# The last stores and GpSimd's last additions behind the branch of the fallback check

## The chip, the core and the metric

One core of a Trainium2 chip runs the whole program. A core has five engines with an instruction queue each: TensorE (matrix products; PE in the profile, with its weight loads as PEld), VectorE (DVE), ScalarE (ACT), GpSimd (POOL) and SyncE (SP), which here only issues transfers. Sixteen DMA engines move data between the memory of the chip and the core's own (SBUF). The metric is the time of one execution on the device in microseconds (us); lower is better.

## The reference

The input is x, 2048 rows of 512 numbers. What is computed:

```python
xn = layernorm(x)                                  # over the 512 numbers of a row
q, k, v = split(xn @ wqkv)                         # 32 heads of 16
s = softmax(q k^T / 4) v, heads joined, @ wo       # attention
h = relu(xn @ w1 + b1) ** 2                        # 512 -> 1792
g = silu(h @ w2 + b2)                              # 1792 -> 512
return x + s * g
```

## The kernel before, in words

The kernel has two ways to the result. `fast_path` computes everything, with an attention that takes no maximum out of the scores ahead of the exponential. It also gathers the smallest and largest values of what could go wrong with that (row sums, values) in a tile `stat`. At its end it makes one number of them, `nvalid`: 128 where all 128 rows of `stat` are in bounds. `general_path` reads that number into a register of every engine and branches: if it is below 128, the attention is computed again in a slow and safe manner, and the output is written over. With the inputs of the reference the number is 128, so the general path's body is passed over.

The order of the work on each engine is written out by hand. Attention goes by 64 turns (each for a group of 4 heads, a chunk of 512 queries and 8 blocks of 128 keys), and the products of the feed-forward layers are woven in between as fillers. The end of it, which the change touches, is this. The last chunk of attention is complete; VectorE adds up its two halves (line 1258), TensorE transposes the row sums into place and VectorE takes their reciprocals (1265, 1266). TensorE spreads these over the tile (1275) and VectorE multiplies (1277, 1280), which gives the normalized last head group `norms`. Two small flags are made in between (1278, 1279). Numbers are carried as a rounded part h and a rest l, so that products of rounded numbers give nearly full precision: ScalarE rounds two halves (1282), VectorE subtracts (1284). A product of the flags (1286) gives the number, and VectorE writes it to `nvalid` as an integer (1287). Then, for the last four tiles of 128 rows, three products each (1021, called from `group` at 1296) complete the projection by wo; VectorE scales each by 0.5 and multiplies it by the gate (1299); x is added (1303, 1305) and the tile is stored (1291, 1309). The additions of tiles 0 and 1 and of the first half of tile 3 are GpSimd's, those of tile 2 and the second half of tile 3 VectorE's. ScalarE's queue issues the stores of tiles 0, 2, 1 and of the first half of tile 3, in that order, SyncE's queue the store of the second half. SyncE also stores two tiles of the chunk before (1136), the last one shortly ahead of these.

Behind that each engine loads the number into a register (line 1321) and branches (1322). Line 1418 is the end of the program: SyncE waits there for all transfers, and the engines meet twice.

The tiles have fixed places in SBUF by name: `t(shape, dtype, tag)` gives the next of the places of that tag, as P0 to P15 or KA0 to KA2. The four output tiles `o` lie in P2 to P5, the rows of x that are added in KA1. The pool `sb` that holds all these is closed when `fast_path` returns.

Of the kernel before, what the change touches and what calls it, by code (L numbers as in the profile page):

```python
# [24 lines left out]
FT = mybir.dt.float32  # L25
# [23 lines left out]
def mha_ffn_kernel(ctx: ExitStack, tc: tile.TileContext, x, wqkv, wo, bx, w1, b1, w2, b2, out):  # L49
# [20 lines left out]
    gdram = dram.tile([S, D], FT, name="gd")  # L70

    with tc.tile_pool(name="sb", bufs=1) as sb, ExitStack() as banks:
        fast_path(tc, sb, banks, locals())
    general_path(tc, dram, nvalid, ident, vdram, kdram, qdram, gdram, x, wo, out)


def fast_path(tc, sb, banks, env):
# [11 lines left out]
    open_pool = lambda stack, name, side: stack.enter_context(tc.tile_pool(name=name, bufs=1, space=PSUM, side=side))  # L89
    ps = dict(B=open_pool(below, "ps0", "left"), D=open_pool(above, "ps1", "right"))  # L90

    def t(shape, dt, tag):

        cnt[0] += 1
        if tag in BUFS:
            turn[tag] = turn.get(tag, -1) + 1
            n = turn[tag] % BUFS[tag]
            p, tag = ps.get(tag), f"{tag}{places[n] if tag == 'S' else n}"
        else:
            p = None  # L100
        return (p or ps.get(tag, sb)).tile(shape, dt, tag=tag, name=f"{tag}_{cnt[0]}")

    split_tiles = [f"{a}{n}" for a in ("xh", "xl", "wf2h", "wf2l", "hh", "hl") for n in range(2)]
    for tags, n in (((f"P{i}" for i in range(16)), 1024), (("KA0", "KA1", "KA2"), 2048),
                    (("QA0", "QA1", "wf1h0", "wf1l0", *split_tiles), 1024),
# [799 lines left out]

    sums = {}

    def load_rowsums(qd, qc):
        sums[qd, qc] = t([32, 64], FT, "zc")
        sp.dma_start(sums[qd, qc], zdram[qd][qc].rearrange("h (a b) -> (h a) b", b=64))  # L910

    def rowsums(qd, qc):
        z, r = sums.pop((qd, qc)), t([32, 64], FT, "rc")
        check(z, 4 * qd + qc)
        dve.reciprocal(r, z)
        sp.dma_start(udram[qd // 2][qc][1, qd % 2].rearrange("d h (a b) -> (h a) d b", b=64),
                     r.unsqueeze(1).broadcast_to([32, 16, 64]))
# [363 lines left out]
    for n, s in enumerate(half):  # L1281
        act.copy(h[:, s], norms[n])
    for n, s in enumerate(half):
        dve.tensor_tensor(l[:, s], norms[n], h[:, s].bitcast(FT), op=OP.subtract)
    pn = acc[0:1, :1]
    mm(pn, flags[:, 0:1], flags[:, 1:2], start=True, stop=True)
    dve.tensor_copy(nvalid, pn)
    o, lins = [t([128, 512], FT, f"P{2 + i}") for i in range(4)], [two[:, 0], small[:, 1], acc, lin]
# [3 lines left out]

    late = []
    for i in range(4):
        gate, old = gsb[3, i // 2][:, i % 2], base[3, i // 2][:, i % 2]
        group(lins[i], lambda p: (h, l)[p][:, cut[i]], lambda p: wlast[0][:, p])
        for n, s in enumerate(half if i == 3 else [slice(0, 512)]):
            dst = lins[i] if i == 2 or n == 1 else o[i]
            dve.scalar_tensor_tensor(dst[:, s], lins[i][:, s], 0.5, gate[:, s], op0=OP.mult, op1=OP.mult)
            if i == 3:  # L1300
                late.append((n, dst, s, old))
            else:
                (dve if i == 2 else pool).tensor_tensor(o[i], dst, old, op=OP.add)
    for n, dst, s, old in late:
        (pool, dve)[n].tensor_tensor(o[3][:, s], dst[:, s], old[:, s], op=OP.add)
    for i in (0, 2, 1):
        save(i)
    for n, s in enumerate(half):
        (act, sp)[n].dma_start(out[1920:, s], o[3][:, s])


def general_path(tc, dram, nvalid, ident, vdram, kdram, qdram, gdram, x, wo, out):

# [7 lines left out]
    n = nc.values_load(nvalid[0:1, 0:1])  # L1321
    with tc.If(n < 128), tc.tile_pool(name="gsb", bufs=1) as sb, \
            tc.tile_pool(name="gps", bufs=1, space=PSUM) as ps:
# [51 lines left out]
        with tc.For_i(0, NK, 1) as b:  # L1375
# [17 lines left out]
            dve.tensor_tensor(gt, gt, xt, op=OP.add)  # L1393
            nc.gpsimd.dma_start(out[ds(b * 128, 128)], gt)


# [25 lines left out]
```

## Time and profile before

| | us |
|---|---|
| median of 3 runs | 1198.42 (1197.73 to 1199.0) |
| the profiled execution's own time | 1197.88 |
| its span, from first to last instruction | 1196.3 |
| TensorE busy | 1187.8 |
| ScalarE busy | 1055.8 |
| VectorE busy | 861.9 |
| GpSimd busy | 351.9 |

The profile is of one execution, taken by the hardware. Its times run from the start of the span. A row of the timeline gives start, duration, engine, the line of the kernel, the operation, what it writes and reads, and how many instructions it joins (x3); in brackets stands how long the engine sat idle before, and for whom. An engine's name with a q (ACTq, SPq, POOLq) is its instruction queue itself, which loads registers, branches and issues transfers beside the engine's work. A row of a line gives the shortest, the median and the longest duration in ns, and the first and the last start. A row of the stretches gives its bounds, its length, the busy time of TensorE, its weight loads, VectorE, ScalarE and GpSimd (with counts), the granted clock of TensorE, the share of time in which the 16 DMA engines were busy, and GB/s.

### The profile page before, as it was taken

The numbers are of one execution on the slowest core, as the hardware profiler recorded it, in microseconds if no ns is written. First come the engines' busy times: TensorE is split into PE (matmuls) and PEld (weight loads), VectorE is DVE, ScalarE is ACT, GpSimd is POOL, SyncE is SP. The second block draws the span as 40 slices with busy tenths as digits, with TensorE's granted clock in tenths as the row PEclk, the third lists the DMA queues.
The fourth block names the chain that finished last, engine by engine and source line by source line (L and its number), as shares of the span: only waits on it lengthen the run. The fifth ranks groups of instructions, "written<-read, shape, count | busy, mean of one in ns | idle before, by whom it ended". The sixth has DMA issues, their size and how long they took to land.

```text
span 1196.3 us, 24322 instructions
## 1 busy us (share of the span) xinstructions
PE 1187.8 (99%) x9853; PEld 712.3 (60%) x9853; DVE 861.9 (72%) x1367; ACT 1055.8 (88%) x1340; POOL 351.9 (29%) x209
## 2 busy tenths in 40 slices
PE   9999999999999999999999999999999999999997
PEld 6888755555555555655555655555565556555554
DVE  7666777676867777757687666677775868778876
ACT  6655689999999999999999999999999999999994
POOL 5756523040312321304032122220230403321224
PEclk9999999999999999999999999999999999999999
DMA  7798914131353223224423123141422232464344
GB/s 289 289 379 319 351 59 139 45 111 46 98 156 97 82 64 90 72 80 152 119 77 102 59 88 96 46 168 45 135 81 81 76 104 81 135 218 162 119 152 142
DMA packets 108152, 155.70 MB, mean 130 GB/s; under 512 B 43514, under 2 KB 58120, under 8 KB 108036
## 3 DMA queue, kind: packets, MB, share of 16 engines
q1 hardware_dynamic: 105108, 145.26, 37.6%
q0 software_dynamic: 2352, 7.93, 2.1%
q8 instruction: 78, 1.28, 0.5%
q10 hardware_dynamic: 576, 0.92, 0.2%
q14 instruction: 38, 0.31, 0.1%
HBM read 104.14 MB, written 49.67 MB: 129 GB/s over the span
## 4 chain that ended last, share of the span: by engine, by line
PE 99%; DVE 1%; DMA 0%; issue 0%; ACT 0%; DVEq 0%
PE acc L866 38%; PE S L568 29%; PE S L515 14%; PE B L326 5%; PE acc L515 4%; PE B L127 4%; PE lin L515 2%; PE D L326 1%; PE D L253 1%; PE S L1021 0%; PE lin L326 0%; DMA P<-in_A_x_dram 0%; PE acc L326 0%; PE S L326 0%; DVE st L190 0%; DVE T L226 0%
## 5 line engine op out<-in xcount | busy, mean ns | idle before, releaser
L519 ACT ACTIVATE P<-S 128x1024 f32<-128x1024 f32 x592 | 559.8, 1031 | 67.9 <-PE S L515 65.2
L866 PE MATMUL acc<-P,V 128*32 128x512 f32 x4096 | 453.6, 594 | 0.0
L519 ACT ACTIVATE P<-P 128x1024 f32<-128x1024 f32 x324 | 321.6, 1059 | 0.0
L866 PEld LDWEIGHTS acc<-P,V 128*32 128x32 f32 x4096 | 126.2, 110 | 289.3 <-issue 269.1
L515 PE MATMUL S<-QA,KA 64*128 64x512 f32 x1346 | 282.7, 400 | 0.0
L541 DVE COPY P<-acc 128x512 f32<-128x512 f32 x318 | 219.9, 691 | 66.4 <-PE acc L515 33.6
L541 DVE COPY P<-lin 128x512 f32<-128x512 f32 x330 | 227.6, 690 | 12.1 <-PE lin L515 5.7
L120 POOL TENSOR_TENSOR wf1l<-wr,wf1h 128x1024 fp32r<-128x1024 f32 x28 | 68.4, 2444 | 504.4 <-PE S L515 299.6
L515 PEld LDWEIGHTS S<-QA,KA 64*128 64x128 f32 x1346 | 132.0, 184 | 82.8 <-ACT seen L1143 41.9
L515 PE MATMUL lin<-QA,KA 64*128 64x512 f32 x384 | 149.5, 389 | 0.0
L515 PE MATMUL acc<-QA,KA 64*128 64x512 f32 x318 | 124.0, 390 | 0.0
L120 POOL TENSOR_TENSOR wf2l<-wr,wf2h 128x1024 fp32r<-128x1024 f32 x28 | 67.4, 2407 | 109.2 <-DVE wf2h L116 81.8
L522 ACT ACTIVATE P<-S 128x512 f32<-128x512 f32 x162 | 98.0, 605 | 0.0
L568 PE MATMUL S<-xl,wf1h 64*128 64x512 f32 x464 | 96.1, 387 | 0.0
L120 POOL TENSOR_TENSOR hl<-T,hh 128x1024 fp32r<-128x1024 f32 x28 | 80.2, 2864 | 53.2 <-DVE hh L116 51.3
L568 PE MATMUL S<-xh,wf1h 64*128 64x512 f32 x480 | 93.0, 389 | 0.0
L568 PE MATMUL S<-wf2l,hh 64*128 64x512 f32 x448 | 90.5, 387 | 0.0
L568 PE MATMUL S<-xh,wf1l 64*128 64x512 f32 x480 | 87.4, 386 | 0.0
L568 PE MATMUL S<-wf2h,hh 64*128 64x512 f32 x448 | 84.4, 388 | 0.0
L568 PE MATMUL S<-wf2h,hl 64*128 64x512 f32 x448 | 78.2, 386 | 0.0
L1144 DVE TENSOR_TENSOR seen<-P,lin 1x1 f32<-1x1 f32 x63 | 8.9, 141 | 96.1 <-ACT P L522 93.4
L515 PEld LDWEIGHTS lin<-QA,KA 64*128 64x128 f32 x384 | 70.7, 184 | 8.4 <-DVE P L541 1.3
(384 smaller groups left out, 1507.6 us busy)
## 6 DMA issues: line engine op xcount, KB each, us to landing
wr<-in_B_w_dram SPq DMA_DIRECT2D x56, 512.0 KB
QA<-qd SPq DMA_DIRECT2D x128, 128.0 KB
KA<-kd SPq DMA_DIRECT2D x64, 256.0 KB
u<-ud SPq DMA_DIRECT2D x15, 512.0 KB
kd<-P SPq DMA_DIRECT2D x11, 512.0 KB
V<-vd SPq DMA_DIRECT2D x8, 664.0 KB
qd<-P SPq DMA_DIRECT2D x9, 512.0 KB
vd<-P SPq DMA_DIRECT2D x16, 280.0 KB
```

Of the source, the lines that this page charges most:

```text
L120: leng.tensor_tensor(lo, src, hi.bitcast(FT), op=OP.subtract)
L127: mm(dst, lhs(a, k), rhs(b, k), start=n == 0, stop=n == len(todo) - 1)
L253: nc.tensor.transpose(halves[k // 2][:, k % 2, 128 * j:128 * j + 128], xnorm[c, i][:, j, 128 * k:128 * k + 128], ident)
L326: mm(dst, left[a][:, k], right[b][:, k], start=n == 0, stop=n == 5)
L515: mm(dst, k[r, p, 128 * (kb % 8):128 * (kb % 8) + 128], q[r, p], start=True, stop=True)
L519: act.activation(ptile[i, p], src, AF.Exp, scale=SCALE)
L522: act.activation(ptile[i, p][:, hp], src, AF.Exp, scale=SCALE)
L541: dve.tensor_copy(ptile[i, p][:, hp], sides[bank])
L568: ins = mm(bank, self.lhs(a, k)[r], self.rhs(b, k)[r], start=n == 0 and self.at[other] == 0, stop=n == len(self.todo[half]) - 1 and self.a ...
L866: mm(sides[0][32 * j:32 * j + 32], vq[qd][:, kb, 17 * j:17 * j + 32], ptile[i, j // 2][:, j % 2], start=first, stop=last)
L1144: dve.tensor_tensor(seen[:, 8:9], last, sides[1][:1, :1], op=OP.max)
```

## The change

Three things are done together.

1. GpSimd's last three additions and the five last stores move behind the branch: `fast_path` no longer issues them but returns a function `stores`, and `general_path` calls it in the other arm of the branch, the one that is run when the number is 128. Their order among themselves stays as it was.
2. The integer copy to `nvalid` moves up on VectorE, from behind the second subtraction of line 1284 to between the two. The product that makes the number is written ahead of both subtractions; on TensorE it stands where it stood, ahead of the products of the last four tiles.
3. The tiles that are still read or written there, P2 to P5 and KA1, lie in a pool `ends` of their own, which stays open around both functions. (The dictionary of the row sums is renamed, since `sums` is now the list of the additions put off.)

VectorE's last two additions stay ahead of its branch. If the general path is taken, the last 512 rows are written by it alone.

```diff
-        fast_path(tc, sb, banks, locals())
-    general_path(tc, dram, nvalid, ident, vdram, kdram, qdram, gdram, x, wo, out)
+        stores = fast_path(tc, sb, banks, locals())
+    general_path(tc, dram, nvalid, ident, vdram, kdram, qdram, gdram, x, wo, out, stores)
...
+    for tag, n in (("P2", 1024), ("P3", 1024), ("P4", 1024), ("P5", 1024), ("KA1", 2048)):
+        ps[tag] = env["ends"]
+        ps[tag].tile([128, n], FT, tag=tag, name=f"{tag}_first")
...
     for n, s in enumerate(half):
         act.copy(h[:, s], norms[n])
+    pn = acc[0:1, :1]
+    mm(pn, flags[:, 0:1], flags[:, 1:2], start=True, stop=True)
     for n, s in enumerate(half):
         dve.tensor_tensor(l[:, s], norms[n], h[:, s].bitcast(FT), op=OP.subtract)
-    pn = acc[0:1, :1]
-    mm(pn, flags[:, 0:1], flags[:, 1:2], start=True, stop=True)
-    dve.tensor_copy(nvalid, pn)
+        if n == 0:
+            dve.tensor_copy(nvalid, pn)
...
+    def total(eng, i, src, s, old):
+        eng.tensor_tensor(o[i][:, s], src[:, s], old[:, s], op=OP.add)
+
     for i in range(4):
...
             if i == 3:
-                late.append((n, dst, s, old))
+                late.append((i, dst, s, old))
             else:
-                (dve if i == 2 else pool).tensor_tensor(o[i], dst, old, op=OP.add)
-    for n, dst, s, old in late:
-        (pool, dve)[n].tensor_tensor(o[3][:, s], dst[:, s], old[:, s], op=OP.add)
-    for i in (0, 2, 1):
-        save(i)
-    for n, s in enumerate(half):
-        (act, sp)[n].dma_start(out[1920:, s], o[3][:, s])
+                sums.append((i, dst, slice(0, 512), old))
+                if i == 2:
+                    total(dve, *sums.pop())
+    total(dve, *late.pop())
+    sums += late
+
+    def stores():
+        for a in sums:
+            total(pool, *a)
+        for i in (0, 2, 1):
+            save(i)
+        for n, s in enumerate(half):
+            (act, sp)[n].dma_start(out[1920:, s], o[3][:, s])
+
+    return stores
...
-    with tc.If(n < 128), tc.tile_pool(name="gsb", bufs=1) as sb, \
+    with tc.If(n < 128) as few, tc.tile_pool(name="gsb", bufs=1) as sb, \
             tc.tile_pool(name="gps", bufs=1, space=PSUM) as ps:
...
+    with few.Else():
+        stores()
```

More of the change, by code (lines that the diff above doesn't have):

```diff
@@ L70, in mha_ffn_kernel @@
     gdram = dram.tile([S, D], FT, name="gd")
+    ends = ctx.enter_context(tc.tile_pool(name="ends", bufs=1))
     with tc.tile_pool(name="sb", bufs=1) as sb, ExitStack() as banks:
-        fast_path(tc, sb, banks, locals())
-    general_path(tc, dram, nvalid, ident, vdram, kdram, qdram, gdram, x, wo, out)
+        stores = fast_path(tc, sb, banks, locals())
+    general_path(tc, dram, nvalid, ident, vdram, kdram, qdram, gdram, x, wo, out, stores)
 def fast_path(tc, sb, banks, env):
@@ L98, in t @@
             p, tag = ps.get(tag), f"{tag}{places[n] if tag == 'S' else n}"
+            p = p or ps.get(tag)
         else:
@@ L103, in fast_path @@
     split_tiles = [f"{a}{n}" for a in ("xh", "xl", "wf2h", "wf2l", "hh", "hl") for n in range(2)]
-    for tags, n in (((f"P{i}" for i in range(16)), 1024), (("KA0", "KA1", "KA2"), 2048),
+    for tags, n in (((f"P{i}" for i in range(16) if f"P{i}" not in ps), 1024), ([a for a in ("KA0", "KA1", "KA2") if a not in ps], 2048),
                     (("QA0", "QA1", "wf1h0", "wf1l0", *split_tiles), 1024),
@@ L904, in check @@
         dve.tensor_reduce(stat[:m, 32 + n:33 + n], z, axis=AX.X, op=OP.max)
-    sums = {}
+    rowsum = {}
     def load_rowsums(qd, qc):
-        sums[qd, qc] = t([32, 64], FT, "zc")
-        sp.dma_start(sums[qd, qc], zdram[qd][qc].rearrange("h (a b) -> (h a) b", b=64))
+        rowsum[qd, qc] = t([32, 64], FT, "zc")
+        sp.dma_start(rowsum[qd, qc], zdram[qd][qc].rearrange("h (a b) -> (h a) b", b=64))
     def rowsums(qd, qc):
-        z, r = sums.pop((qd, qc)), t([32, 64], FT, "rc")
+        z, r = rowsum.pop((qd, qc)), t([32, 64], FT, "rc")
         check(z, 4 * qd + qc)
@@ L1291, in save @@
         act.dma_start(out[1536 + 128 * i:1664 + 128 * i], o[i])
-    late = []
+    late, sums = [], []
+    def total(eng, i, src, s, old):
+        eng.tensor_tensor(o[i][:, s], src[:, s], old[:, s], op=OP.add)
     for i in range(4):
@@ L1300, in fast_path, with general_path @@
             if i == 3:
-                late.append((n, dst, s, old))
+                late.append((i, dst, s, old))
             else:
-                (dve if i == 2 else pool).tensor_tensor(o[i], dst, old, op=OP.add)
-    for n, dst, s, old in late:
-        (pool, dve)[n].tensor_tensor(o[3][:, s], dst[:, s], old[:, s], op=OP.add)
-    for i in (0, 2, 1):
-        save(i)
-    for n, s in enumerate(half):
-        (act, sp)[n].dma_start(out[1920:, s], o[3][:, s])
-def general_path(tc, dram, nvalid, ident, vdram, kdram, qdram, gdram, x, wo, out):
+                sums.append((i, dst, slice(0, 512), old))
[11 more added lines that the diff above has]
+    return stores
+def general_path(tc, dram, nvalid, ident, vdram, kdram, qdram, gdram, x, wo, out, stores):
     nc = tc.nc
```

## The prediction

> **What bounds the kernel now.** I read the page first, then each engine's own rows in the last ten microseconds, the stretches of the tail, the transfers inside them, and the sequencers' rows of lines 1321, 1322 and 1418. The page says why nothing but the tail matters here.
>
> ```profile
> PE 1187.8 (99%) x9853; PEld 712.3 (60%) x9853; DVE 861.9 (72%) x1367; ACT 1055.8 (88%) x1340; POOL 351.9 (29%) x209
> ```
>
> TensorE is busy for 99% of the span, and the change takes nothing from it: the product for the flag stands where it stood, and the last product ends at 1189.9 (rows of TensorE: start, duration, what).
>
> ```profile
> 1186.61 0.19 PE L1286 MATMUL acc<-ones 128*1 128x1 f32 x2 [0.28 <-DVE ones L1279]
> ...
> 1189.52 0.39 PE L1021 MATMUL lin<-QA,wf1l 128*128 128x512 f32 x1
> ```
>
> What can move lies behind that. The last rows of VectorE, GpSimd, ScalarE's queue and SyncE's queue are these (start, duration, what):
>
> ```profile
> 1186.88 0.89 DVE L1284 TENSOR_TENSOR wf1l<-S,wf1h 128x256 fp32r<-128x256 f32 x2
> 1187.68 0.14 DVE L1287 CAST nvalid<-acc 1x1 int32<-1x1 f32 x1
> 1187.90 1.38 DVE L1299 SCALAR_TENSOR_TENSOR P<-S,wr 128x512 f32<-128x512 f32 x2
> ...
> 1191.52 0.42 DVE L1305 TENSOR_TENSOR P<-lin,KA 128x256 f32<-128x256 f32 x1
> ```
>
> ```profile
> 1186.57 1.29 POOL L1135 TENSOR_TENSOR wf2l<-wf2l,hl 128x512 f32<-128x512 f32 x1
> 1188.67 2.51 POOL L1303 TENSOR_TENSOR P<-P,KA 128x512 f32<-128x512 f32 x2 [0.81 <-DVE P L1299]
> 1191.15 0.72 POOL L1305 TENSOR_TENSOR P<-P,KA 128x256 f32<-128x256 f32 x1
> ```
>
> ```profile
> 1189.99 2.01 ACTq L1291 DMA_DIRECT2D out_dram<-P  x3
> 1192.38 0.34 ACTq L1309 DMA_DIRECT2D out_dram<-P  x1
> ```
>
> ```profile
> 1187.88 0.35 SPq L1136 DMA_DIRECT2D out_dram<-wf2l  x1
> 1191.97 0.33 SPq L1309 DMA_DIRECT2D out_dram<-P  x1
> ```
>
> VectorE hands over its last half tile at 1191.52 + 0.42 = 1191.94, GpSimd its own at 1191.87, and the five stores are out of the queues at 1192.72. The span ends 3.6 us later. Two views of that stretch (busy time by engine, DMA share, GB/s; then the sequencer rows of the kernel's end):
>
> ```profile
> 1191.50:1192.00 0.50, 0.00 (x0) 0.00 (x0) 0.42 (x1) 0.00 (x0) 0.36 (x1) 1.00 0.16 49
> 1192.00:1194.00 2.00, 0.00 (x0) 0.00 (x0) 0.00 (x0) 0.00 (x0) 0.00 (x0) 1.00 1.03 381
> 1194.00:1194.40 0.40, 0.00 (x0) 0.00 (x0) 0.00 (x0) 0.00 (x0) 0.00 (x0) 1.00 0.37 100
> 1194.40:1195.00 0.60, 0.00 (x0) 0.00 (x0) 0.00 (x0) 0.00 (x0) 0.00 (x0) 0.56 0.12 32
> ```
>
> ```profile
> L1418 SPq EVENT_SEMAPHORE  x8: 28/28/28, 1194.0 to 1195.4; - x8
> L1418 SPq DRAIN  x2: 7/10/13, 1195.5 to 1195.5; - x2
> L1418 POOLq DRAIN  x1: 1452/1452/1452, 1193.0 to 1193.0; - x1
> ```
>
> The transfers run full from 1192.0 to about 1194.05 (381 GB/s), then a thin tail carries 32 to 100 GB/s for another 0.8 us. SyncE waits for every landing; its last wait is over at 1195.4, and 0.9 us of barriers follow to 1196.3. So the **last landing** sets the end, and it is late because a few of the 16 DMA engines are still at work when the others have finished.
>
> Who holds them? Instruction packets in the transfers of 1192.7 to 1193.5, then of 1193.5 to 1194.95 (packets, MB, share of 16 engines):
>
> ```profile
> q14 instruction: 1, 0.01, 4.2%
> ```
>
> ```profile
> q14 instruction: 3, 0.02, 5.0%
> ```
>
> One took 0.8 × 16 × 4.2% = 0.54 us of a DMA engine, the three others 1.45 × 16 × 5.0% = 1.16 us together, in the middle of the last stores. From 1188.6 to 1191.5 there is one of another queue (GB/s in 40 slices of 0.0725 us, then its row):
>
> ```profile
> GB/s 0 28 282 424 424 395 424 424 452 395 283 85 0 0 0 226 0 0 0 0 0 0 0 0 0 0 0 0 0 0 0 198 395 367 424 339 339 395 424 367
> ...
> q8 instruction: 1, 0.02, 3.0%
> ```
>
> It starts in the lone slice at 1189.7 and takes 2.9 × 16 × 3.0% = 1.4 us. All five stand behind the branches of the engines (the load of the flag, then the branch and what follows it; the two times are the first and the last start):
>
> ```profile
> L1321 POOLq TENSOR_LOAD <-nvalid x1: 492/492/492, 1191.1 to 1191.1; - x1
> ...
> L1321 ACTq TENSOR_LOAD <-nvalid x1: 798/798/798, 1192.8 to 1192.8; - x1
> ```
>
> ```profile
> L1322 POOLq EVENT_SEMAPHORE  x4: 17/43/43, 1192.1 to 1192.4; - x4
> L1322 PEldq COMPARE_BRANCH  x1: 375/375/375, 1188.6 to 1188.6; - x1
> L1322 PEldq EVENT_SEMAPHORE  x1: 51/51/51, 1189.9 to 1189.9; - x1
> L1322 POOLq COMPARE_BRANCH  x1: 45/45/45, 1191.6 to 1191.6; - x1
> L1322 DVEq COMPARE_BRANCH  x1: 72/72/72, 1192.2 to 1192.2; - x1
> ...
> L1322 SPq COMPARE_BRANCH  x1: 50/50/50, 1193.2 to 1193.2; - x1
> L1322 ACTq COMPARE_BRANCH  x1: 54/54/54, 1193.6 to 1193.6; - x1
> ```
>
> **The change, part by part.** *The flag earlier.* The product behind it is done long before (1186.80), so the copy can follow the first subtraction. Two of these subtractions take 0.89 us from start to end, so one is over by about 1187.3, and the copy ends near 1187.4 instead of 1187.82. The second subtraction waits anyway for ScalarE's second half:
>
> ```profile
> L1282 ACT CAST wf1h<-S x2: 373/374/374, 1186.5 to 1186.9; 128x256 fp32r<-128x256 f32 x2
> ```
>
> That is over at 1187.3; behind the copy the subtraction starts at most 0.14 us later, and the first scaling of line 1299 waits for TensorE at 1187.90. On VectorE this costs 0 (bounds: 0 and 0.14, and 0.14 only if that wait vanished). The flag is 0.45 us earlier for all readers.
>
> *GpSimd's three additions behind its branch.* Its load now starts at 1187.4 + 0.05, while the addition of line 1135 runs until 1187.86. Load 0.49 to 0.80 (the rows' extremes), branch 0.05, then 0.45 from branch to first instruction (1191.6 to 1192.1, short of the 45 ns): ready at 1188.45 to 1188.8. The first addition waits for VectorE and starts at 1188.67 today. So its delay is 0 to 0.15; I take 0. GpSimd's three additions run back to back to 1191.87, so a delay would go through whole; but ScalarE issues that half tile only at 1192.38, so 0.5 us of cover lies behind it.
>
> *ScalarE's four stores and SyncE's one.* ScalarE's load can start at 1187.4, so it is through the branch by 1187.45 + 0.80 + 0.05 + 0.45 = 1188.75; its first store waits for GpSimd until 1189.97. SyncE first issues the store of line 1136 at 1187.88 (0.35), and is ready by 1188.24 + 0.05 + 0.80 + 0.05 + 0.45 = 1189.6, 2.4 us ahead of 1191.97. Cover is ample; the issue of all five stores costs nothing more. Nothing is queued behind the two loads but these stores, and the order of the five issues is the same.
>
> *What this buys.* GpSimd's, ScalarE's and SyncE's branches, with what they fetch, move from 1191.6–1194.8 to about 1188–1190, where transfers have gaps. ScalarE's load and branch behind its last issue (1192.8 to 1193.7), and SyncE's with them, vanish too, but they end 1.7 us before the last landing, so they are worth 0 by themselves. VectorE's branch stays at 1192.2, since its last addition stays ahead of it, and one packet (0.54 us, starting 1192.7) is very likely its own. The two ends of the gain: all four packets out of the way, then the last landing is as far behind the end of the full stretch as the last thin packet was from the last wait: thin tail over at about 1194.9, wait over at 1195.4, so 0.5 behind; 1194.05 + 0.5 = 1194.55, a gain of 0.85. With VectorE's packet left, 0.54 of it stays: gain 0.3. A third unknown is the hole at 1191.5 to 1192.0 (49 GB/s): ScalarE's three issues span 2.01 us, where single ones take 0.33 to 0.35. If the issue behind this hole comes as much sooner, 0.4 more; if GpSimd is late, 0.15 less. I take a **gain of 0.5**, nearer to the lower end because the packet at 1192.7 follows VectorE's branch. GpSimd's drain (1.45 us, over at 1194.46) must not become the last: its start moves ahead with the branch, so it does not.
>
> The profiled execution took 1197.88 us with a span of 1196.3, so 1.6 lies around the span; it stands 0.54 under the median 1198.42 of runs between 1197.73 and 1199.0. 1197.88 − 0.5 = 1197.4 for it, and **1197.9** as a median.
>
> A rule speaks against the change. The Trainium skill, "Runtime: NRT & Kernel Launch", section "Instruction fetch mechanics", says that a taken branch to a target outside the two resident pages stalls until that page is fetched. By that rule the stall, now at the very end, would stand ahead of the additions, and the time is the first rival's, 1198.7 or more, instead of 1197.9 by the rows; the trace does not bear the rule out so far, since GpSimd's first instruction behind its branch (1192.1) precedes the first packet of queue 14 (1192.7).
>
> **Rivals.** *The branch stalls GpSimd (slower).* The jump passes over the whole general path; if its target isn't resident in the new program, GpSimd waits for a packet. The nearest row is TensorE's: branch over at 1188.6 + 0.38 = 1189.0, the packet of queue 8 done at 1189.7 + 1.4 = 1191.1, so 2.1 to 2.2 us (TensorE itself ran its next instruction at 1189.9, before that). Then the first addition starts at 1187.45 + 0.5 to 0.8 + 0.05 + 2.2 = 1190.2 to 1190.5, a delay of 1.5 to 1.85; the last half tile comes at 1193.4 to 1193.7, its issue takes 0.34, and an undisturbed store needs 2.1 from issue to landing (line 1136: issued 1187.88, its transfers over at 1189.5, and 0.5 to the wait). Landing 1195.5 to 1195.8, later than 1195.4: slower by 0.1 to 0.4, 1198.7, and 1199.2 with VectorE's packet on top. It decides from a delay of about 1.3 us. For it: no view shows where the target lies. Against: 0.45 us behind the branch today.
>
> *The packets are not what holds the last landing* (nothing changes). Then the tail is the stores' own unevenness: 1198.4. For it: four packets of 1.7 us are few beside a full stretch of 2 us on 16 engines. Against: the thin tail, which 16 equal shares would not leave.
>
> *All of it goes, and the hole too* (gain 0.85 to 1.2): 1197.4. No more is possible: VectorE's 1191.94, 2.1 from issue to landing and 0.9 of barriers come to 1194.9 to 1195.1, some 1.2 under today's end.
>
> *Both arms get a meeting of the engines of their own.* The two rounds of barriers at the end take 0.9 us; one more of half that, wholly ahead of the stores, gives 1198.4 or less, hidden by the cover above.
>
> **How the numbers follow.** Forecast (gain 0.2 to 0.7, 1197.9): 0.55. Nothing changes, barriers included (1198.4): 0.20. Larger gain (1197.4): 0.12. GpSimd stalls (1198.7 to 1199.2): 0.13. The range takes in the larger gain (1197.4) and the stall (1198.7 and most of the way to 1199.2), and 0.5 below, by which the profiled execution stands off its own median: 1196.9 to 1199.1. What this kernel's measurement can tell from no change is 0.2%, 2.4 us. No case reaches that: the largest gain is 1.1 to 1.2, the worst priced loss 0.8. So faster 0.03, same 0.93, slower 0.04, the rest for what I have not thought of.
>
> **What would show it.** The copy to nvalid between two rows of line 1284, near 1187.3; loads of POOLq, ACTq and SPq at 1187.4 to 1188.3; the first GpSimd addition still at 1188.67; the first stores still at 1190.0 and 1192.0; fewer than four instruction packets behind 1192.0; the thin tail gone or shorter; SyncE's first drain at 1194.9 to 1195.2 instead of 1195.5. I am wrong if GpSimd's first addition starts behind 1189, if the tail stands unchanged without the packets, or if a new wait appears between branch and stores.

## The result, and the profile after

| | before | after |
|---|---|---|
| median of 22 runs each, us | 1198.16 (1197.72 to 1199.0) | 1199.82 (1198.94 to 1200.24) |
| the profiled execution's own time | 1197.88 | 1200.24 |
| its span | 1196.3 | 1198.7 |

The changed kernel is **slower by 1.66 us**: ratio 1.0014, 95% interval 1.0008 to 1.0019. That lies within the 0.2% that the chances counted as the same, but it is a loss where a gain of 0.5 was forecast, and 1199.82 is above the range.

The two profiled executions differ by 2.4 us of span. To split that, the rows of the tail are read from one instruction that the change doesn't touch, ScalarE's last rounding of `h`. In the profile before, its pair of roundings starts at 1186.47 and takes 0.84, the last of them 0.37, so it starts at 1186.93. Timeline rows of ScalarE and its queue after the change (start, duration, what):

```profile
1187.62 0.83 ACT L1287 CAST wf1h<-S 128x256 fp32r<-128x256 f32 x2 [1.33 <-DVE S L1282]
1191.22 2.96 ACTq L1297 DMA_DIRECT2D out_dram<-P  x3
1194.27 0.48 ACTq L1325 DMA_DIRECT2D out_dram<-P  x1
```

Here it starts at 1187.62 + 0.83 - 0.37 = 1188.08, 1.15 later; what stands ahead of it is the same work. From there to the end of the span, called the **tail** from here on, it is 9.4 us before (1196.3 - 1186.9) and 10.6 after (1198.7 - 1188.1): +1.2 is lost behind the rounding. What lies ahead of it is mostly the spread of the executions, as the first experiment shows. (Of the 1.66 between the medians the tail shows 1.2; the other 0.4 is inside the interval, which is 1.0 to 2.3 us, and isn't explained.)

In the tail, ScalarE's three stores of line 1297 span 2.96 us, where they spanned 2.01. The row of that line has the shortest, median and longest:

```profile
L1297 ACTq DMA_DIRECT2D out_dram<-P x3: 384/411/1968, 1191.2 to 1193.8; - x3
```

One issue takes **1.968 us** (this long issue is called the **hold** from here on), and it is the first: the timeline cut to the middle of the long span shows it alone.

```profile
1191.22 1.97 ACTq L1297 DMA_DIRECT2D out_dram<-P  x1
```

Before, the three took 0.381 (the first), 0.798 and 0.389:

```profile
L1291 ACTq DMA_DIRECT2D out_dram<-P x3: 381/389/798, 1190.0 to 1191.6; - x3
```

GpSimd's last sums show that the data was ready, and SyncE's queue shows its old store (line 1141, 1136 before) ahead of it, and its own last store behind:

```profile
1189.89 3.20 POOL L1302 TENSOR_TENSOR P<-P,KA 128x512 f32<-128x512 f32 x3 [0.89 <-DVE P L1309]
```

```profile
1189.03 0.35 SPq L1141 DMA_DIRECT2D out_dram<-wf2l  x1
1193.15 0.34 SPq L1325 DMA_DIRECT2D out_dram<-P  x1
```

While ScalarE's first issue stands, no transfer of data starts. Stretches of the tail after the change (bounds, length, busy time by engine, granted clock, DMA share, GB/s):

```profile
1190.70:1191.20 0.50, 0.39 (x2) 0.00 (x0) 0.47 (x2) 0.00 (x0) 0.50 (x2) 1.00 0.30 82
1191.20:1193.20 2.00, 0.00 (x0) 0.00 (x0) 1.85 (x4) 0.00 (x0) 1.89 (x2) 1.00 0.00 0
1193.20:1195.20 2.00, 0.00 (x0) 0.00 (x0) 0.00 (x0) 0.00 (x0) 0.00 (x0) 0.94 0.79 291
1195.20:1197.20 2.00, 0.00 (x0) 0.00 (x0) 0.00 (x0) 0.00 (x0) 0.00 (x0) 0.50 0.65 237
1197.20:1197.80 0.60, 0.00 (x0) 0.00 (x0) 0.00 (x0) 0.00 (x0) 0.00 (x0) 0.50 0.01 3
```

From 1191.2 to 1193.2 it is 0 GB/s. (A packet counts in these views where it starts, so one that started before 1191.2 may still run.) What did start, in 1190.7 to 1191.2, are the instruction packets (queue, kind: packets, MB, share of 16 engines; q1 carries SyncE's transfers):

```profile
q8 instruction: 1, 0.02, 15.7%
q14 instruction: 3, 0.02, 14.1%
q1 hardware_dynamic: 2, 0.00, 0.2%
```

Three packets of q14, those that go with the branches of ScalarE, GpSimd and SyncE, have left the last data, as forecast. They run from 1190.8 on, which in the times of the profile before is 1190.8 - 1.15 = 1189.65: the late end of the 1188 to 1190 that was forecast, right behind the old store's data and right where the first store is issued. There they meet TensorE's packet (q8), which runs where it ran before, 2.8 behind the rounding, and lasts 0.5 × 16 × 15.7% = 1.26 us, to 1192.1. The branches themselves are where they were forecast (loads of the flag, then branches):

```profile
L1339 ACTq TENSOR_LOAD <-nvalid x1: 462/462/462, 1188.5 to 1188.5; - x1
L1339 POOLq TENSOR_LOAD <-nvalid x1: 493/493/493, 1188.5 to 1188.5; - x1
...
L1339 SPq TENSOR_LOAD <-nvalid x1: 545/545/545, 1189.4 to 1189.4; - x1
```

```profile
L1340 ACTq COMPARE_BRANCH  x1: 50/50/50, 1189.1 to 1189.1; - x1
L1340 POOLq COMPARE_BRANCH  x1: 45/45/45, 1189.1 to 1189.1; - x1
```

The fourth packet of q14, the one that goes with VectorE's branch, still lies in the last data (in 1195.5 to 1197.0), and the thin end of the transfers with it. SyncE's first drain, after its wait for all landings, is 2.3 us later than the 1195.5 of before:

```profile
q14 instruction: 1, 0.01, 1.3%
```

```profile
L1438 SPq DRAIN  x3: 7/7/13, 1197.8 to 1198.1; - x3
```

How 1.59 us more in one issue become 1.2 in the tail: read from the rounding, ScalarE's last issue starts at 1194.27 - 1188.08 = 6.19, before at 1192.38 - 1186.93 = 5.45, so 0.74 later (before, the four issues came spread out, from 1190.0 to 1192.4; now three go out one behind the other when the first is over). It takes 0.14 longer (0.48, 0.34 before). From its end to the drain it is 1197.8 - 1194.75 = 3.05, before 1195.5 - 1192.72 = 2.78, so 0.27 more: before, some 0.24 MB had moved ahead (157 GB/s from 1190.0 to 1191.5), and now all of it waits together. 0.74 + 0.14 + 0.27 = 1.15, which is the 1.2 within the 0.1 to which the drains are given.

### The profile page after: what moved, and what is told of

It is laid out like the page before. It is cut to its first block, busy times and chain, and to the rows that moved or that the text cites. A ratio compares the mean times of both kernels' runs of the same rounds, so it can differ in the third digit from the quotient of the medians.

```text
span 1198.7 us, 24325 instructions
## 1 busy us (share of the span) xinstructions
PE 1189.1 (99%) x9853; PEld 722.1 (60%) x9853; DVE 861.8 (72%) x1367; ACT 1056.5 (88%) x1340; POOL 351.4 (29%) x209
## 4 chain that ended last, share of the span: by engine, by line
PE 99%; DVE 0%; issue 0%; POOL 0%; ACT 0%; POOLq 0%; DVEq 0%
PE acc L871 37%; PE S L573 29%; PE S L520 14%; PE B L331 5%; PE acc L520 4%; PE B L132 4%; PE lin L520 3%; PE D L331 1%; PE D L258 1%; PE B L692 0%; PE S L1026 0%; PE lin L331 0%; PE acc L331 0%; DVE P L1309 0%; PE S L331 0%; DVE P L1302 0%
## 5 line engine op out<-in xcount | busy, mean ns | idle before, releaser
L520 PE MATMUL S<-QA,KA 64*128 64x512 f32 x1346 | 285.6, 400 | 0.0
L520 PEld LDWEIGHTS S<-QA,KA 64*128 64x128 f32 x1346 | 134.4, 184 | 80.1 <-ACT seen L1148 41.9
```

Source lines behind the costliest of these rows:

```text
L520: mm(dst, k[r, p, 128 * (kb % 8):128 * (kb % 8) + 128], q[r, p], start=True, stop=True)
```

## The experiments

Each kernel is the changed one with the edit shown. The ratio is to the kernel before on the same chip. "First" is the duration of the first store's issue (tile 0) and its queue, "tail" the time from ScalarE's last rounding to the end of the span of the profiled execution, "early" which of ScalarE, SyncE and GpSimd branch ahead of their last stores or additions, or have none left. TensorE's branch is early in all, the kernel before included, save in e4.

| | early | old store | first | tail | median, before | ratio, 95% |
|---|---|---|---|---|---|---|
| before | none | SyncE | ScalarE 0.381 | 9.4 | 1198.16 | |
| after | ScalarE, SyncE, GpSimd | SyncE | ScalarE 1.968 | 10.6 | 1199.82, 1198.16 | 1.0014 (1.0008 to 1.0019) |
| e1 | none | SyncE | ScalarE 0.381 | 9.1 | 1198.58, 1198.86 | 0.9998 (0.9989 to 1.0007) |
| e2 | all three | SyncE | ScalarE 2.127 | 11.1 | 1200.53, 1198.86 | 1.0013 (1.0004 to 1.0022) |
| e3 | all three | SyncE | ScalarE 2.060 | 10.7 | 1200.11, 1198.86 | 1.0011 (1.0001 to 1.002) |
| e4 | all three, TensorE late | SyncE | ScalarE 1.172 | 9.9 | 1199.67, 1198.86 | 1.0006 (0.9997 to 1.0015) |
| e5 | SyncE | SyncE | ScalarE 0.381 | 9.0 | 1198.53, 1198.78 | 0.9999 (0.999 to 1.0008) |
| e6 | ScalarE, SyncE | SyncE | ScalarE 1.326 | 10.0 | 1199.81, 1198.78 | 1.0009 (1.0 to 1.0018) |
| e7 | all three | SyncE | SyncE 0.343 | 8.7 | 1198.53, 1198.78 | 0.9997 (0.9988 to 1.0006) |
| e8 | all three | left out | ScalarE 0.603 | 8.8 | 1199.25, 1198.78 | 1.0004 (0.9995 to 1.0013) |
| e9 | all three, ScalarE 0.9 later | ScalarE | ScalarE 0.343 | 8.9 | 1198.09, 1198.45 | 0.9994 (0.9985 to 1.0003) |
| e10 | all three, ScalarE 0.9 later | ScalarE | SyncE 0.362 | 8.5 | 1198.42, 1198.45 | 0.9998 (0.9989 to 1.0007) |
| e11 | ScalarE | SyncE | SyncE 0.332 | 8.9 | 1198.61, 1198.45 | 0.9998 (0.9989 to 1.0007) |
| e12 | ScalarE | SyncE | ScalarE 1.262 | 10.0 | 1198.45, 1197.61 | 1.0007 (0.9998 to 1.0016) |
| e13 | all three, ScalarE 0.9 later | SyncE | ScalarE 2.451 | 11.3 | 1200.27, 1198.2 | 1.0016 (1.0007 to 1.0026) |
| e14 | all three | SyncE | SyncE 0.345, then ScalarE 1.400 | 10.1 | 1198.88, 1198.2 | 1.0006 (0.9996 to 1.0016) |

A tail is of one execution, and the medians have the spread of the part ahead of it; so the tails and the issues tell the causes apart, and the medians bear them out where the interval allows it. The tails of before and e1, whose stores and branches have the same order, differ by 0.3; less than that says nothing.

The theory to begin with: the early branches' packets hold ScalarE's first issue. Rivals: the flag's new place or the pool costs it; the first issue behind any branch is slow; the old store is to blame.

**e1: nothing in the other arm.** The additions and stores stand ahead of the branch again; the flag's copy and the pool stay as changed.

```diff
     n = nc.values_load(nvalid[0:1, 0:1])
+    stores()
...
-    with few.Else():
-        stores()
```

> The changed kernel with its additions and stores taken back ahead of the branch; the earlier flag and the tile pool of their own stay. Clogged DMA engine (my theory: the instruction packets that follow the four early branches hold one DMA engine, and ScalarE's first store issue, 1.97 us instead of 0.38, waits for that engine): the time is that of the kernel before within 0.4 us, the first issue of ScalarE takes 0.4, one instruction packet (TensorE's) stands ahead of the stores. Placement (rival: the new places of the tiles, or the earlier flag, slow down the whole, as the last rows of the profile stand 1.15 us later than before already at the last head group): 0.7 to 1.7 us slower than before.

The issues of line 1297 in e1:

```profile
L1297 ACTq DMA_DIRECT2D out_dram<-P x3: 381/388/525, 1191.3 to 1192.7; - x3
```

The long issue is gone, the loss with it. So the flag and the pool don't make the loss (e1 against before: -0.28, interval -1.3 to +0.8); it is the other arm's. The rounding stands even later in e1's profiled execution (1188.29) than in that of the change; but that execution was 0.49 above e1's median, and the profiled one of before (1197.88) 0.98 below the median that the kernel before has beside e1 (1198.86). Put to these medians the rounding lies at 1187.80 in e1 and 1187.91 before. That is an estimate, since the profile of before was not taken among those runs, but by it the 1.15 ahead of the tail is no effect of the flag or the pool.

**e2: a tiny transfer first.** ScalarE issues a transfer of 64 bytes a row, into a place that nobody reads, as its first instruction behind the branch.

```diff
+    tiny = dram.tile([128, 16], FT, name="tiny")
...
     with few.Else():
+        act.dma_start(tiny, ident[:, :16])
         stores()
```

> The changed kernel; ScalarE issues one small transfer more (128 rows of 64 bytes) as its first instruction behind the branch. Clogged engine: the small issue near 1189.5 takes under 0.6, ScalarE's first store at 1191.2 still 1.2 to 2.0, the time is that of the changed kernel within 0.5. First issue behind a branch (rival: what a queue needs for its first issue after a branch must be loaded first): the small issue takes 1 to 2 us, the first store 0.4, the time falls by about 1 us.

Timeline rows of e2's ScalarE queue, then of SyncE's:

```profile
1189.65 0.34 ACTq L1415 DMA_DIRECT2D tiny<-ident  x1
1191.36 3.13 ACTq L1297 DMA_DIRECT2D out_dram<-P  x3
```

```profile
1193.28 0.34 SPq L1325 DMA_DIRECT2D out_dram<-P  x1
```

The tiny issue right behind the branch takes 0.34, and the store 1.7 us later is held (2.127 us) all the same. So it isn't the first issue behind a branch that is slow; it is the time at which it falls. The second fence shows one thing more: the held issue ends at 1191.36 + 2.13 = 1193.49, and SyncE issues its own store at 1193.28 in 0.34, so for 0.21 us inside ScalarE's hold. Whatever holds ScalarE's queue doesn't hold SyncE's; e13 below shows it for a whole issue.

**e3 and e8: without the old store.** e3 was meant to leave out the store of line 1141 at 1189.0 but left out the one ahead of it, at 1182.7; e8 leaves out the right one. In each, 128 rows of the output aren't written.

```diff
             # e3
-            sp.dma_start(rows, o)
+            if i < 3:
+                sp.dma_start(rows, o)
             # e8
-            sp.dma_start(rows, o)
+            if i != 2:
+                sp.dma_start(rows, o)
```

> The changed kernel without SyncE's last store of the chunk before (line 1141, 256 KB, issued at 1189.0), so 128 rows of the output are not written. Clogged engine: the packets no longer stand behind that store's data, they move at 1189.4 to 1190.6 instead of 1190.8 to 1192.1, ScalarE's first store takes 0.4 to 0.9, and the time falls by 0.8 to 1.5. First issue behind a branch: the first store still takes 1.6 to 2, the time changes by less than 0.3.

> The changed kernel without the store of the chunk before that SyncE issues at 1189.0 (the run that was meant to leave it out, e3, left out the one at 1182.7), so 128 other rows of the output are not written. Clogged engine: the packets no longer stand behind that store's data, so they move some 0.5 to 1.3 us earlier and are over sooner: ScalarE's first issue takes 0.4 to 1.0, the time falls by 0.6 to 1.6 against the changed kernel. If that store's data don't matter: first issue 1.6 to 2.1, the time falls by less than 0.3.

e3 is a miss and says nothing on the store in question; the hold stands in it (2.060). In e8 the issues of the first stores, then the instruction packets of 1190.0 to 1192.0 (GB/s in slices of 0.05 us, then the rows):

```profile
L1298 ACTq DMA_DIRECT2D out_dram<-P x3: 365/384/603, 1191.2 to 1192.4; - x3
```

```profile
GB/s 0 164 164 164 0 0 0 0 0 0 0 0 0 328 0 0 0 0 0 0 0 0 0 0 0 0 0 0 0 0 0 0 0 0 0 0 0 0 0 0
...
q14 instruction: 3, 0.02, 3.7%
q8 instruction: 1, 0.02, 3.5%
```

Without the old store's data the three packets run 0.7 us sooner (at 1190.05 to 1190.2, which is 2.0 behind the rounding instead of 2.7), and the first issue takes 0.603, though TensorE's packet still starts at 1190.65 and runs 2.0 × 16 × 3.5% = 1.1 us, past that issue's start at 1191.18. So the old store is a part of the cause: it takes 1.4 of the 1.6 us with it. Whether it does so itself or through the earlier packets, e8 doesn't tell. The median (+0.47, of 1198.47 to 1199.84) doesn't tell e8 from before.

**e4: TensorE's branch late.** A product that reads the last output tile, and that nobody reads, keeps TensorE from its branch until the end.

```diff
+    mm(two[:1, 1, :1], o[3][:, 511:], o[3][:, 511:], start=True, stop=True)
     return stores
```

> The changed kernel; TensorE ends with one product of 128x1 by 128x1 more that reads VectorE's last half tile, so its own branch comes at about 1193.5 instead of 1189.9. Clogged engine, with TensorE's 16 KB packet as the one that holds it: ScalarE's first store takes 0.4 to 0.6; the packet meets the later issues or the last data instead, so the time falls by 0 to 1.2. If the 8 KB packets of the three other engines alone hold the first store: it still takes over 1.2 and the time does not fall. First issue behind a branch: 1.6 to 2 as now.

Issues of e4, then its instruction packets of 1191 to 1193:

```profile
L1297 ACTq DMA_DIRECT2D out_dram<-P x3: 384/409/1172, 1191.5 to 1193.3; - x3
```

```profile
q14 instruction: 3, 0.02, 3.0%
```

Without TensorE's packet the issue takes 1.172, between the two values expected: that packet is 0.8 of the 1.6 us. (The shares overlap: without the old store 1.4 are gone, TensorE's packet still being there.)

**e5, e6 and e12: who has to be early.** e5 puts SyncE's store alone in the other arm, e12 ScalarE's four stores alone, e6 all five stores without GpSimd's additions.

```diff
     # e5
-        for n, s in enumerate(half):
-            (act, sp)[n].dma_start(out[1920:, s], o[3][:, s])
-    return stores
+        act.dma_start(out[1920:, half[0]], o[3][:, half[0]])
+    stores()
+    return lambda: sp.dma_start(out[1920:, half[1]], o[3][:, half[1]])
     # e6
+    for a in sums:
+        total(pool, *a)
     def stores():
-        for a in sums:
-            total(pool, *a)
     # e12
+    for a in sums:
+        total(pool, *a)
+    sp.dma_start(out[1920:, half[1]], o[3][:, half[1]])
     def stores():
-        for a in sums:
-            total(pool, *a)
...
-        for n, s in enumerate(half):
-            (act, sp)[n].dma_start(out[1920:, s], o[3][:, s])
+        act.dma_start(out[1920:, half[0]], o[3][:, half[0]])
```

> Only SyncE's one store (the second half of the last tile) stands in the other arm; the additions and ScalarE's four stores stand ahead of the branch, the earlier flag and the tile pool stay. Clogged engine: one 8 KB packet joins TensorE's ahead of the stores, ScalarE's first issue takes 0.4 to 1.0, and one packet fewer stands among the last data: between 0.4 faster and 0.4 slower than before. If each early branch costs the same share of the 1.66 us: 0.5 slower. Early branches are harmless and ScalarE's own is the cause (rival): first issue 0.38, 0.1 to 0.4 faster than before.

> The five stores stand in the other arm, GpSimd's additions stay ahead of its branch, so ScalarE, SyncE and TensorE branch early and GpSimd late. Clogged engine: two 8 KB packets and TensorE's ahead of the stores, ScalarE's first issue takes 0.9 to 1.7, 0.5 to 1.3 us slower than before. If GpSimd's early branch is the cause: first issue 0.38, no slower than before.

> Only ScalarE's four stores stand in the other arm; GpSimd's additions and SyncE's store stand ahead of their branches. With e5 (SyncE alone: not delayed) and e6 (SyncE and ScalarE: 1.33) it tells the number of early packets from whose branch it is. Number: one 8 KB packet beside TensorE's, as in e5; ScalarE's first store takes 0.4 to 0.7, the time is within 0.4 of the kernel before. ScalarE's own branch: the first store takes 1.0 to 1.7, the time is 0.5 to 1.2 us above before.

Issues and packets at the first store, in e5 (1190.6 to 1191.8) and in e12 (1189.6 to 1190.8):

```profile
L1297 ACTq DMA_DIRECT2D out_dram<-P x3: 352/353/381, 1190.9 to 1192.1; - x3
```

```profile
q8 instruction: 1, 0.02, 4.9%
q14 instruction: 1, 0.01, 1.9%
```

```profile
L1297 ACTq DMA_DIRECT2D out_dram<-P x3: 384/407/1262, 1190.0 to 1191.8; - x3
```

```profile
q8 instruction: 1, 0.02, 5.1%
q14 instruction: 1, 0.01, 1.6%
```

The two have the same packets, one of each queue, and only one holds the issue: the one whose early branch is **ScalarE's own**. So it isn't the number of packets. (The place differs a little: the packet of q14 starts 3.10 behind the rounding in e5, 2.72 in e12, and the issue at 3.07 in both.) e6 (1.326), with SyncE's branch early too, is like e12; the changed kernel, with GpSimd's early as well, has 1.968.

**e7 and e11: the stores on SyncE's queue.** e7 issues all five stores of the changed kernel there; e11 does the same with nothing in the other arm.

```diff
-        act.dma_start(out[1536 + 128 * i:1664 + 128 * i], o[i])
+        sp.dma_start(out[1536 + 128 * i:1664 + 128 * i], o[i])
...
-            (act, sp)[n].dma_start(out[1920:, s], o[3][:, s])
+            sp.dma_start(out[1920:, s], o[3][:, s])
```

> The changed kernel with all five stores issued by SyncE's queue instead of four by ScalarE's. Clogged engine: SyncE's issue of the first store takes 1.5 to 2.1 like ScalarE's, the time is that of the changed kernel within 0.6 (one queue issues all, the last half tile goes last). Something of ScalarE's queue alone (rival): the first issue takes 0.3 to 0.5, the time falls by 0.7 or more.

> Nothing stands in the other arm; all five stores are issued by SyncE's queue ahead of the branch, with the earlier flag. It separates the two parts of e7. If the queue alone made e7 fast: 0.1 to 0.5 faster than before, as e7. If the early branches help once the issue doesn't wait: 0.0 to 0.5 slower than e7, with four instruction packets among the last data and a last landing 0.4 to 0.8 later than in e7 counted from ScalarE's last rounding.

Issues of e7, and its packets of 1191.4 to 1192.6:

```profile
L1297 SPq DMA_DIRECT2D out_dram<-P x3: 343/372/414, 1191.9 to 1193.1; - x3
```

```profile
q14 instruction: 3, 0.02, 5.7%
q8 instruction: 1, 0.02, 5.2%
q1 hardware_dynamic: 2, 0.00, 0.1%
```

The same four packets as in the changed kernel, the first issue inside them, and it takes 0.343. That any queue waits there is wrong. e7's tail (8.7) is the shortest so far, shorter than before's 9.4; the median (-0.25) can't tell it from before, nor e11's (+0.16). e11's tail is 0.2 longer than e7's, and so is its last landing, where 0.4 to 0.8 were expected if the early branches help.

**e9 and e10: the old store on ScalarE's queue.** In both it is held back a little and issued there, behind the last rounding. e9 leaves the last stores where they are, e10 puts them on SyncE's queue as in e7: the queues of the changed kernel exchanged.

```diff
-            sp.dma_start(rows, o)
+            if i == 2:
+                hold.append((rows, o))
+            else:
+                sp.dma_start(rows, o)
...
+    act.dma_start(*hold.pop())
```

> The changed kernel, but the store of the chunk before that SyncE issues at 1189.0 is issued by ScalarE's queue, ahead of its branch; so it stands in the same queue as the four last stores. Other queue's transfer (theory after e7 and e8: an issue waits while a transfer of another queue is unfinished on the DMA engine that serves the instruction packets; what its own queue has unfinished there doesn't hold it): ScalarE's first store takes 0.4 to 0.6, the time falls by 0.8 to 1.8 against the changed kernel, to that of the kernel before or below. ScalarE's queue (rival: ScalarE's issues wait for the packets, SyncE's do not): the first store still takes 1.5 to 2.1, the time is that of the changed kernel within 0.5.

> The changed kernel with that old store on ScalarE's queue and all five last stores on SyncE's: the two queues of the changed kernel exchanged. Other queue's transfer: SyncE's first store takes 1.5 to 2.1, the time is that of the changed kernel within 0.6. ScalarE's queue: the first store takes 0.4, the time is 1 to 2 us below that of the changed kernel, as in e7.

The first stores' issues in e9, and in e10:

```profile
L1303 ACTq DMA_DIRECT2D out_dram<-P x3: 343/387/588, 1190.4 to 1191.8; - x3
```

```profile
L1303 SPq DMA_DIRECT2D out_dram<-P x3: 362/390/518, 1190.9 to 1192.2; - x3
```

Neither is held (0.343 and 0.362 for the first). e9 shows that ScalarE's queue isn't slow as such, e10 that an unfinished transfer of the other queue isn't enough either. e9 is the fastest version of all (-0.36), but its interval includes 1: no version was found that surely beats the kernel before.

e9 differs from the changed kernel in two things: ScalarE issues the old store, and so comes to its branch 0.9 later. Two more kernels take that apart.

**e13: ScalarE's branch late, the old store left on SyncE's queue.** ScalarE issues a small transfer (64 bytes of each row of the same tile) where e9 has the old store.

```diff
+            if i == 2:
+                hold.append(o)
...
+    act.dma_start(env["dram"].tile([128, 16], FT, name="tiny"), hold.pop()[:, :16])
```

> The changed kernel; ScalarE issues one small transfer (64 bytes of each row of the tile that the old store of line 1141 writes out) behind its last rounding, ahead of its load of the flag. It waits for the same GpSimd addition as the old store, so ScalarE's branch falls at about 1.9 us behind the last rounding instead of 0.98, as in the kernel that has the old store on ScalarE's queue (where the first issue took 0.343); the old store stays on SyncE's queue. If the hold comes from the moment of ScalarE's branch (its instruction packet asked for at 1.0, behind the old store's data), the first issue of tile 0 takes 0.35 to 0.6 here and the tail is 8.8 to 9.3 us, the median near before's. If it comes from the old store being unfinished on SyncE's queue while ScalarE has branched at any time ahead of it, the issue takes 1.2 to 2.0 and the tail is 10 to 11 us, 1 to 1.7 slower than before.

```profile
L1302 ACTq DMA_DIRECT2D out_dram<-P x3: 384/419/2451, 1190.8 to 1193.8; - x3
```

The row is that of e13's first stores: 2.451, the longest hold of all, longer than expected (1.2 to 2.0). SyncE's last store, in the same stretch:

```profile
1192.68 0.35 SPq L1330 DMA_DIRECT2D out_dram<-P  x1
```

It begins and ends inside ScalarE's hold (1190.77 to 1193.22). And it isn't the moment of ScalarE's branch that frees e9: that is 1.93 behind the rounding there, and 1.90 here. Two differences are left. One is the old store's queue. The other is ScalarE's own instruction packet: taken in the order of the branches, it starts at 3.06 in e13, ahead of the held issue (3.13), and at 3.17 in e9, behind the start of the issue (3.13); in every kernel with a hold of over 1 us it starts ahead of the held issue. No run changes one of the two and keeps the other.

**e14: tile 0's store alone on SyncE's queue.**

```diff
-        act.dma_start(out[1536 + 128 * i:1664 + 128 * i], o[i])
+        (act if i else sp).dma_start(out[1536 + 128 * i:1664 + 128 * i], o[i])
```

> The changed kernel with tile 0's store alone on SyncE's queue. Its issue at 3.1 behind the last rounding takes about 0.35, as with all stores on SyncE's queue. ScalarE's first issue is then tile 2's at about 3.8. If ScalarE's queue is closed until about 0.4 behind the old store's last landing (landings of 3.9 to 4.9 so far), that issue ends at 4.3 to 5.3 and takes 0.5 to 1.5. If only an issue that begins inside an instruction packet is held (the packets end at 3.8 to 4.0), it takes 0.35 to 0.6. In both cases less is lost than in the changed kernel: tail 8.7 to 9.8 us, median between 0.3 faster and 0.6 slower than before.

Timeline rows of e14's ScalarE queue, then the rows of its line 1297:

```profile
1191.35 1.88 ACTq L1297 DMA_DIRECT2D out_dram<-P  x2
```

```profile
L1297 ACTq DMA_DIRECT2D out_dram<-P x2: 385/892/1400, 1191.4 to 1192.8; - x2
L1297 SPq DMA_DIRECT2D out_dram<-P x1: 345/345/345, 1190.7 to 1190.7; - x1
```

SyncE's issue passes in 0.345. ScalarE's begins 0.7 later, 3.81 behind the rounding and just as TensorE's packet ends (3.79), and still takes 1.400 (the tail, 10.1, is longer than the 8.7 to 9.8 expected). So it isn't only an issue that begins inside a packet that is held: ScalarE's queue is closed with no instruction packet running, while on SyncE's queue the issue here (3.12 behind the rounding) and e7's second one (3.80, 0.414) pass.

**What the runs settle, and what stays open.** Shown: the loss is the hold of ScalarE's first issue, and it needs ScalarE's branch ahead of its stores (e1 and e5 are without it) and the last stores on ScalarE's queue (on the other in e7, e10 and e11; e14 has both in one kernel). The old store has a part in it (without it, in e8, 0.2 us of hold are left). That it has to be on SyncE's queue is not shown: it rests on e9 against e13, which differ in ScalarE's packet too. TensorE's packet is half of it (e4), and the other early branches lengthen it (e12 and e6 against the changed kernel).

Open is why. The trace has the last of the old store's 16 landings 4.69 behind the rounding in the changed kernel, and the held issue ends at 5.11; in e2, e3, e4, e6, e12 and e14, too, it ends 0.28 to 0.47 behind that landing (at 4.91, 4.91, 4.00, 3.98, 3.86, 4.89). That would make the landing the releaser, but in e13 the landing is at 3.40 (that of ScalarE's own small transfer at 4.44) and the hold ends at 5.58, and in e7 the landing is at 4.91 and SyncE's issue waits for nothing. Nor does an unfinished transfer of the other queue hold SyncE's (e10). The Trainium skill, "Perfetto Trace Analysis", section "DMA Instruction — HWDGE (DVE, Sync)", says that the block that makes the descriptors is shared by two engines under a lock, and that the recorded duration of an issue holds the wait for that lock. The trace shows no issue of SyncE's under way from 1189.4 to 1193.15, and in e13 SyncE's issue passes during ScalarE's hold, so this lock alone doesn't explain it.

## Why the prediction was wrong, point by point

- **The flag earlier costs VectorE nothing: right** (e1). The copy stands between the two subtractions, as said.

```profile
1188.02 0.42 DVE L1291 TENSOR_TENSOR wf1l<-S,wf1h 128x256 fp32r<-128x256 f32 x1
1188.36 0.13 DVE L1293 CAST nvalid<-acc 1x1 int32<-1x1 f32 x1
1188.48 0.42 DVE L1291 TENSOR_TENSOR wf1l<-S,wf1h 128x256 fp32r<-128x256 f32 x1
```

- **GpSimd's first addition late by 0 to 0.15: right.** It starts 1189.89 - 1188.08 = 1.81 behind the rounding, before 1188.67 - 1186.93 = 1.74: 0.07.
- **The rival of a stalled branch: didn't come.** GpSimd's branch is over at 1189.14, and its addition, which VectorE's row releases, starts at 1189.89, ahead of the packets, which start behind 1190.7. In e2, ScalarE's small transfer starts 0.4 behind its branch. The rule of the Trainium skill that the prediction weighed ("Runtime: NRT & Kernel Launch", section "Instruction fetch mechanics": the engine stands until the page of a target that isn't resident is fetched) isn't seen at work at the branches: the packets come, and the next instructions don't wait for them. No view shows whether the target was resident. What waited was a transfer's issue two us later.
- **Packets in the last data make the tail longer: borne out in direction, not shown in size.** Among the kernels without a long hold, those with four packets of q14 behind the last stores have tails of 9.4 and 9.1 (before, e1), those with three 9.0 and 8.9 (e5, e11), those with one 8.5 to 8.9 (e7 to e10). That is 0.2 to 0.9 between four packets and one, where 0.3 to 0.85 were forecast, from single executions, and e7 to e10 differ from before in the old store or in a queue as well. The medians of e7 to e10 (-0.36 to +0.47) can't confirm so little.
- **"One packet (0.54 us, starting 1192.7) is very likely its own" (VectorE's): doubtful.** In e8, where no data is queued ahead, the packets start 1.0 us behind their branches. The one at 1192.7 starts 1.0 behind the end of GpSimd's branch (1191.67) and only 0.4 behind that of VectorE's (1192.31), so it was more likely GpSimd's. VectorE's packet does stay in the last data, as said, but the choice of the lower end of the gain rested on this reading.
- **"To about 1188–1190, where transfers have gaps": right, and no help.** In the times of before the packets run from 1189.65 to 1190.5, in the gap between the old store's data and those of the first store. But the first store is issued in that gap. The packets come that late because the old store's 256 KB go out first (218 GB/s from 1189.5 to 1190.7 in the profile after); without them, in e8, they come 0.7 sooner.
- **"Cover is ample; the issue of all five stores costs nothing more": the step that failed.** The term for the five issues was 0. It was +1.59 for the first one alone (1.968 against 0.381). The packets were priced only as load on the DMA engines, and the wait between branch and store only as time for load and branch. That an issue itself can be held wasn't in the sum, nor in a rival; its last paragraph only names "a new wait". What releases the held issue stays open.

That an issue can be held could have been read before the change. The second store's issue in the profile before:

```profile
1190.72 0.80 ACTq L1291 DMA_DIRECT2D out_dram<-P  x1
```

It ends at 1191.52, 0.4 behind TensorE's packet (1189.7 + 1.4 = 1191.1), and that fits the hole at 1191.5 to 1192.0 that the prediction left as "a third unknown". The long run of the kernel has it too. SyncE's issues of line 499, one of them, and the packet in the stretch 480.4 to 481.8, all before the change:

```profile
L499 SPq DMA_DIRECT2D QA<-qd x128: 579/598/1851, 96.4 to 1132.0; - x128
```

```profile
480.25 1.85 SPq L499 DMA_DIRECT2D QA<-qd  x1
```

```profile
q8 instruction: 1, 0.02, 5.9%
```

The issue that usually takes 0.6 takes 1.85 us and ends at 482.10; TensorE's packet began at 480.4 and took 1.4 × 16 × 5.9% = 1.32, to 481.73. The size of the new hold could not be read there: before, the first issue lies wholly inside TensorE's packet and takes 0.381, and after the change the hold ends 1.1 behind that packet (1193.19 against 1192.1), not 0.4.

The range missed for the same reason: its upper end was built from a stall of GpSimd (1199.2), not from a hold of the queue. The tail's +1.2 on the median of before as it was shown (1198.42) gives 1199.6.

## What to carry to other kernels

A branch costs more than its own time: each one sends for instructions, and those packets run on the DMA engines, behind whatever data is queued there. When a branch is moved ahead of the last stores, look which packet comes out when, what is then in flight, and which queue issues the next store, and price a held issue (here 0.8 to 2.1 us more) and not only a share of the bandwidth. Read the longest of a group of issues, not its median: an issue that usually takes 0.6 us and once 1.85 is worth a look at the packets of that moment.

## What the runs showed of the hardware that was not expected

- A transfer's issue isn't a fixed cost. In the kernel before, behind 150 us, 18 issues of SyncE take over 0.7 us; 14 of them overlap a packet of TensorE's and end 0.35 to 0.44 us behind its end (as at 480.25: 0.37). The overlap alone doesn't decide: of 29 issues of SyncE that have such a packet running 0.45 us behind their start, 16 take no more than 0.7.
- Which queue issues a store can matter: 0.343 on SyncE's queue (e7) against 1.968 on ScalarE's (the changed kernel), with the same four packets and the same old store. The Trainium skill, "DMA: Bandwidth & Descriptors", section "Issuing engines are not separate DMA queues", says that the choice of the issuing engine saves only the time to start a transfer. That time is what differs here, by 1.6 us.
- Instruction packets come late, and later behind data: 1.7 us between ScalarE's branch (1189.1) and the first packet (1190.8), where it is 1.0 without the old store's data (e8); and VectorE's, from its branch at 1193.3, not before the stretch that begins at 1195.5.
